# A recurrent attention kernel in which TensorE does one more matmul on constants after four groups of every step

## The chip, the cores and the metric

The kernel runs on one core of a Trainium2 chip. The metric is the time of one execution on the device, in microseconds (us): 1889.78 us is the median of three runs before the change (1886.13 to 1891.63).

## The reference

Two parts follow each other. The first is a recurrence over 768 positions, for 4 batches of 8 heads, on a 40 x 40 state; the second is a mixture of 8 experts on 3072 tokens of 320 numbers, in which all experts are computed for all tokens and weighted with a matrix that is normalised by rows and columns eight times. All is fp32.

```python
for t in range(S):
    y[:, :, t] = np.einsum('bhd,bhde->bhe', rt, state)
    Sa = np.einsum('bhde,bhe->bhd', state, at)
    state_decay = state * wt[:, :, None, :] - np.einsum('bhd,bhe->bhde', Sa, bt)
    state = state_decay + np.einsum('bhd,bhe->bhde', vt, kt)
...
x = np.ascontiguousarray(attn_out.transpose(0, 2, 1, 3)).reshape(B * S, H * D)
...
for e in range(E):
    h = np.maximum(x @ w1[e], 0.0)
    ye = h @ w2[e]
    out += P[:, e:e + 1] * ye
```

## The kernel before

**The attention** cuts the 768 positions into 12 chunks of 64. A *step* is one chunk of one batch, so there are 48. A step treats the 8 heads as 4 pairs, and each of its matmul groups is 4 matmuls (or transposes), one per pair, into one PSUM bank. The function `recur` (L235 to L302) issues a step:

- `av` (L251): the incoming state against the positions; VectorE masks it into `f` (L252)
- `xc` (L259): two groups, `xc0` and `xc1`, in a bank each; ScalarE copies them to `x1` and `c1` (L265, L266)
- `pu` (L270): `x1` through the inverted triangular matrix `tt`; VectorE masks it into `pm` (L272)
- `c2` (L277): `pm` through `bb`; VectorE adds `c1` to give `ws` (L279); GpSimd makes `y`, which goes to memory (L281), and `z`, the outgoing state (L292; on VectorE from chunk 9 on)
- `zt` (L297): `z` transposed; ScalarE copies it to `vz` (L299, L300), the incoming state of the batch's next chunk. The last chunk has none, so there are 44 of these.

These banks come from one pool of 4 (`PC`). A group of 4 x 104 columns fills 416 of a bank's 512 fp32 columns.

Around the steps stand other jobs: the loads and scans of a step's inputs and two more matmul groups, `ll` (L145) and `kt` (L153), in `prep`; the inversion of the triangular matrices on VectorE, for two chunks of all batches at a time (`inv_diag`, `inv_off`, `contract`, L170 to L182); `tload` and `tmat`, which complete the inverse with short matmuls `gp` (L226) and `op` (L231); and the experts' gate `lp` (L307), one short matmul at a time between those of `xc`.

What sets the order: a list of events sorted by due time (L346 to L382) issues the jobs, with the four batches staggered by `SKEW`; then a scheduler, which works on a model of the engines' times, lays down each engine's order. Every engine runs its order strictly. So an instruction more on TensorE also shifts what the scheduler puts where, on every engine.

**The experts** follow (from L450): matmuls at L545 and L610, with ScalarE and VectorE between them. From its eighth block on (`N_MAN`) this part has its order written out by hand.

The constants are in `cst`, [128, 660], which is loaded once at the start; its columns 232 to 359 are the identity.

Of the kernel before, what the change touches and what calls it, by code (L numbers as in the profile page):

```python
# [11 lines left out]
F32 = mybir.dt.float32  # L12
# [8 lines left out]
NP = 4  # L21
R2 = 104
# [6 lines left out]
def attention(ctx, tc, d, xd, ps, pq, pt, gs, lg):  # L29
    nc = tc.nc  # L30
    pin = ctx.enter_context(tc.tile_pool(name="a_in", bufs=1))
    inv = ctx.enter_context(tc.tile_pool(name="a_inv", bufs=1))
    sets = [ctx.enter_context(tc.tile_pool(name=f"a_set{i}", bufs=1)) for i in range(NSX)]
    const = ctx.enter_context(tc.tile_pool(name="a_const", bufs=1))
# [4 lines left out]
    cst = const.tile([128, 64 + 64 + 104 + 128 + 40 + 260], F32, name="cst")  # L39
# [7 lines left out]
    NTB = 2  # L47
    sx_b, bb_b, g_b, cc_b = ([None] * NSX for _ in range(4))
    raws = {}
    for n in range(NCH * NB - NSX, NCH * NB):  # L50
        i, pool = n % NSX, sets[n - NCH * NB + NSX]
        if i in IN_SETS or i in KB_SETS:
# [28 lines left out]
    def clear():  # L81
# [4 lines left out]
        for t in tt_b:  # L86
            nc.gpsimd.memset(t, 0.0)
    fresh = set(range(NSX))

# [9 lines left out]
    def rot(key, lst):  # L99
        i = state[key]  # L100
        state[key] = (i + 1) % len(lst)
        return lst[i]
# [3 lines left out]
    def prep(c, b, ld):  # L106
# [12 lines left out]
        sx = rot("sx", sx_b)  # L119
        i = next(j for j in range(NSX) if sx_b[j] is sx)  # L120
        g, bb, cc = g_b[i], bb_b[i], cc_b[i]
# [97 lines left out]
    def tmat(c, half):  # L219
# [12 lines left out]
        nc.scalar.copy(out=tt[0:32, :, 32:64], in_=op[0:32])  # L232
        nc.scalar.copy(out=tt[64:96, :, 96:128], in_=op[32:64])

    def recur(c, b):  # L235
        pp = preps[c, b]
        vz, zc = vz_cur[b], zp[b]
        nc.sync.dma_start(out=vz[:, :, 0:64], in_=d["v"][c, b])
        rb = io.tile([R2, NP, 128], F32, name="rb", bufs=NRB)
        nc.sync.dma_start(out=rb, in_=d["r"][c, b])  # L240
        f = wk.tile([R2, NP, 2, 104], F32, name="f", bufs=NFB)
        nc.sync.dma_start(out=f[0:64].rearrange("s p h x -> s (p h) x")[:, :, 64:104],
                          in_=d["vt"][c, b].rearrange("s (g x) -> s g x", x=40))
        if zc is None:
            nc.gpsimd.memset(f[64:104].rearrange("s p h x -> s (p h) x")[:, :, 64:104], 0.0)
        else:
            nc.scalar.copy(out=f[64:104, :, 0, 64:104], in_=zc[0:40])
            nc.scalar.copy(out=f[64:104, :, 1, 64:104], in_=zc[64:104])
        av = ps.tile([R2, NP, 2, 64], F32, name="av", tag="ps")
        for p in range(NP):  # L250
            nc.tensor.matmul(av[:, p], lhsT=vz[:, p], rhs=rb[:, p], start=True, stop=True)  # L251
        nc.vector.tensor_tensor(  # L252
            out=f[:, :, :, 0:64], in0=av,
            in1=mask_f.unsqueeze(1).unsqueeze(1).broadcast_to([R2, NP, 2, 64]), op=ALU.mult)
        yield
        xc = [ps.tile([R2, NP, 104], F32, name=f"xc{h}", tag="ps") for h in range(2)]
        for h in range(2):
            for p in range(NP):
                nc.tensor.matmul(xc[h][:, p], lhsT=pp["sx"][:, p, h], rhs=f[:, p, h], start=True, stop=True)  # L259
                if p % 2:  # L260
                    gate_step()
        x1 = wk.tile([128, NP, 104], F32, name="x1")
        c1 = rot("c1", c1_b)
        for h in range(2):
            nc.scalar.copy(out=x1[h * 64:h * 64 + 64], in_=xc[h][0:64])  # L265
            nc.scalar.copy(out=c1[h * 64:h * 64 + 40], in_=xc[h][64:104])  # L266
        yield
        pu = ps.tile([128, NP, 104], F32, name="pu", tag="ps")
        for p in range(NP):
            nc.tensor.matmul(pu[:, p], lhsT=tts[c][:, b * NP + p], rhs=x1[:, p], start=True, stop=True)  # L270
        pm = wk.tile([128, NP, 104], F32, name="pm")
        nc.vector.tensor_tensor(out=pm, in0=pu, in1=mask_p.unsqueeze(1).broadcast_to([128, NP, 104]),  # L272
                                op=ALU.mult)
        yield
        c2 = ps.tile([R2, NP, 104], F32, name="c2", tag="ps")
        for p in range(NP):
            nc.tensor.matmul(c2[:, p], lhsT=pp["bb"][:, p], rhs=pm[:, p], start=True, stop=True)  # L277
        ws = wk.tile([R2, NP, 104], F32, name="ws")
        nc.vector.tensor_tensor(out=ws, in0=c2, in1=c1, op=ALU.add)  # L279
        y = wk.tile([R2, NP, 64], F32, name="y", bufs=NY)  # L280
        nc.gpsimd.tensor_tensor(out=y, in0=ws[:, :, 0:64], in1=pp["g"], op=ALU.mult)  # L281
        col = (b % 2) * 192 + (c % 3) * 64
        tok = (c // 3) * 768 + (col // 128) * 256 + (b // 2) * 128 + col % 128
        for h in range(2):
            nc.sync.dma_start(
                out=xd[h * 160:h * 160 + 160].rearrange("(p e) t -> e p t", e=40)[:, :, tok:tok + 64],
                in_=y[h * 64:h * 64 + 40])
        gq.append(gate(c, b, y))
        if c + 1 == NCH:
            return  # L290
        z = wk.tile([R2, NP, 40], F32, name="z", bufs=4)
        (nc.vector if c >= 9 else nc.gpsimd).tensor_tensor(out=z, in0=ws[:, :, 64:104],  # L292
                                in1=preps[c + 1, b]["cc"].unsqueeze(2).broadcast_to([R2, NP, 40]), op=ALU.mult)
        yield
        zt = ps.tile([40, NP, 104], F32, name="zt", tag="ps")
        for p in range(NP):
            nc.tensor.transpose(zt[:, p], z[:, p], ident[0:R2, 0:R2])  # L297
        vz = rot("vz", vz_b)
        nc.scalar.copy(out=vz[0:40, :, 64:104], in_=zt[:, :, 0:40])  # L299
        nc.scalar.copy(out=vz[64:104, :, 64:104], in_=zt[:, :, 64:104])  # L300
        zp[b] = z
        vz_cur[b] = vz  # L302

    def gate(c, b, y):
        lp = pt.tile([64, E], F32, name="lp", tag="pt")
        for p in range(NP):
            nc.tensor.matmul(lp, lhsT=y[:, p], rhs=gs[:, p], start=(p == 0), stop=(p == NP - 1))  # L307
            if p < NP - 1:
                yield
        col = (b % 2) * 192 + (c % 3) * 64  # L310
        o = col % 128
        nc.vector.tensor_copy(out=lg[o:o + 64, c // 3 * NT + b // 2 * 3 + col // 128], in_=lp)
        yield

    def gate_step():
        if len(gq) > GL:
            next(gq[0])
            gcount[0] += 1
            if gcount[0] % NP == 0:
                gq.popleft()  # L320
# [27 lines left out]
    def step(c, b):  # L348
        if (c, b) not in gens:
            gens[c, b] = recur(c, b)  # L350
        next(gens[c, b], None)
# [6 lines left out]
    for c in range(NCH):  # L358
        for b in range(NB):
            for k in range(5):  # L360
                ev.append((5 * c + k + SKEW * b, step, (c, b)))
        t = 5 * c + 2 - T_LEAD
        ev.append((t - L_LEAD, tload, (c,)))
        for half in range(2):
            ev.append((t + 2 * SKEW * half, tmat, (c, half)))
    for s, cs in enumerate(GROUPS):
# [3 lines left out]
        for i in range(n):  # L370
            cb = (cs[0] + i // NB, i % NB)
            j = cb[0] * NB + cb[1] - NSX
            t = 5 * (j // 4) + 3 + SKEW * (j % 4) + 0.01
            t = max(t, t0 + P0 + PD * i) if s else -20 + 0.01 * i
# [16 lines left out]
PD = 0.75  # L391
INV_DT = 0.05
SKEW = 1.1
NSX = 17
GL = 3
NY = 4
# [32 lines left out]
def body(ctx, tc, d, out):  # L429
# [12 lines left out]
    with ExitStack() as actx:  # L442
        ps, pq, pt = (actx.enter_context(tc.tile_pool(name=f"a_ps{i}", bufs=n, space=bass.MemoryType.PSUM))
                      for i, n in enumerate((PC, PQ, PT)))
        nc.sync.dma_start(out=gs, in_=d["gate"])
        attention(actx, tc, d, xd, ps, pq, pt, gs, lg)
        nc.gpsimd.memset(ones, 1.0)
        nc.sync.dma_start(out=ident, in_=d["cst"][:, 232:360])
# [361 lines left out]
```

## Time and profile before

| | |
|---|---|
| median of three runs | 1889.78 us (1886.13 to 1891.63) |
| the profiled execution | 1890.4 us, span 1888.6 us, mean granted TensorE clock 0.944 |
| TensorE matmuls busy | 1768.8 us (94%), 12035 records |
| VectorE busy | 1397.3 us (74%) |
| ScalarE busy | 854.1 us (45%) |
| GpSimd busy | 876.9 us (46%) |

A span is the time from the first to the last instruction of the profiled execution; the rest of its time lies around it. The profile calls TensorE's matmuls PE and its weight loads PEld, VectorE DVE, ScalarE ACT and GpSimd POOL. Busy time of PE counts a matmul from start to modelled end, so neighbours overlap; what a matmul costs in a row of them is the distance from one start to the next. A matmul of fp32 leaves two matmul records, a transpose one. The granted clock is what share of TensorE's full speed the throttle let through: here it is always 1.0 or 0.5. In a row of waits stand who waited, for whom, the sum in us, how often, and the longest. In a row of the chain of waits stand start, length, and the number of records.

### The profile page before, as it was taken

Reading aid. Unit: us, or ns where it says so; the run is one execution under the profiler, and the core shown is the slowest. Engines: PE = TensorE matmul, PEld = TensorE weight load, DVE = VectorE, ACT = ScalarE, POOL = GpSimd, SP = SyncE. Lnnn points to the kernel's source line nnn. Section 1 sums busy time; section 2 is a strip of 40 time slices with the busy share of each in tenths; the row PEclk is TensorE's granted clock in tenths of the full one; section 3 lists DMA queues with packets and bytes.
Section 4 is the critical chain, followed back from the end, with each engine's and each line's share of the span. In section 5 each row is a group of like instructions: output and inputs, shape, how many; then the busy total and the mean of one; then the engine's idle time right before and its main releaser. Section 6 shows DMA issues by size and latency. Waiting matters only on the chain.

```text
span 1888.6 us, 31821 instructions
## 1 busy us (share of the span) xinstructions
PE 1768.8 (94%) x12035; PEld 1731.0 (92%) x12035; DVE 1397.3 (74%) x2330; ACT 854.1 (45%) x1845; POOL 876.9 (46%) x845
## 2 busy tenths in 40 slices
PE   4468989899898999999999999999999999999999
PEld 4367888889888999999999999999999999999999
DVE  7767767696579877776867777886776767777676
ACT  5346656665563444343433434345343433434342
POOL 6535445542255255371835528004462826537170
PEclk8569968988899999999999999999999999999999
DMA  8567766865642011110201102111110201111011
GB/s 191 100 133 151 151 140 134 166 137 119 147 117 70 23 51 37 37 56 19 73 21 53 52 22 74 55 33 37 37 55 19 73 19 55 37 37 56 18 37 42
DMA packets 187838, 136.26 MB, mean 72 GB/s; under 512 B 155941, under 2 KB 165285, under 8 KB 187685
## 3 DMA queue, kind: packets, MB, share of 16 engines
q1 hardware_dynamic: 184485, 128.98, 27.8%
q10 hardware_dynamic: 3200, 5.25, 1.1%
q8 instruction: 95, 1.56, 0.4%
q14 instruction: 58, 0.48, 0.1%
HBM read 113.74 MB, written 20.45 MB: 71 GB/s over the span
## 4 chain that ended last, share of the span: by engine, by line
PE 76%; DVE 7%; issue 2%; DMA 2%; POOL 1%; ACT 1%; SPq 0%; DVEq 0%; POOLq 0%; ACTq 0%
PE op L610 35%; PE p L545 32%; PE xc L259 2%; PE pu L270 1%; PE av L251 1%; PE ll L145 1%; PE c L277 1%; PE lp L307 1%; PE gp L226 1%; PE op L231 1%; DVE hl L569 1%; DVE un L182 1%; DVE gt L182 1%; PE zt L297 0%; DMA rb<-in_r_dram 0%
## 5 line engine op out<-in xcount | busy, mean ns | idle before, releaser
L545 PE MATMUL p<-xch,wh 128*128 128x384 f32 (+1 forms) x1792 | 605.0, 339 | 5.2 <-DVE cs L654 1.8
L566 ACT ACTIVATE hh<-sm 128x384 fp32r<-128x384 f32 x512 | 269.5, 526 | 726.5 <-DVE sm L563 726.5
L610 PE MATMUL op<-wh,hh 128*128 128x320 f32 x1536 | 477.4, 311 | 1.0 <-ACT hh L566 0.9
L610 PE MATMUL op<-wl,hh 128*128 128x320 f32 x1536 | 474.9, 310 | 0.0
L610 PE MATMUL op<-wh,hl 128*128 128x320 f32 x1536 | 468.1, 310 | 4.4 <-DVE hl L569 4.3
L491 POOL TENSOR_TENSOR wl<-ws,wh 128x640 fp32r<-128x640 f32 x60 | 103.3, 1721 | 608.4 <-ACT wh L489 608.2
L569 DVE SCALAR_TENSOR_TENSOR hl<-sm,hh 128x384 fp32r<-128x384 f32 x512 | 370.9, 758 | 2.8 <-ACT hh L566 2.5
L545 PEld LDWEIGHTS p<-xch,wh 128*128 128x128 f32 (+1 forms) x1792 | 337.5, 188 | 8.5 <-DVE u L563 2.7
L545 PE MATMUL p<-xcl,wh 128*128 128x384 f32 x896 | 302.8, 338 | 0.0
L545 PE MATMUL p<-xch,wl 128*128 128x384 f32 x896 | 302.2, 337 | 0.0
L610 PEld LDWEIGHTS op<-wh,hh 128*128 128x128 f32 x1536 | 290.6, 189 | 1.6 <-ACT hh L566 1.5
L610 PEld LDWEIGHTS op<-wh,hl 128*128 128x128 f32 x1536 | 287.2, 188 | 5.4 <-DVE hl L569 5.2
L610 PEld LDWEIGHTS op<-wl,hh 128*128 128x128 f32 x1536 | 291.5, 190 | 0.0
L563 DVE TENSOR_TENSOR sm<-p,u 128x384 f32<-128x384 f32 x384 | 232.8, 616 | 9.2 <-PE p L545 0.4
L545 PEld LDWEIGHTS p<-xcl,wh 128*128 128x128 f32 x896 | 168.8, 188 | 0.0
L545 PEld LDWEIGHTS p<-xch,wl 128*128 128x128 f32 x896 | 168.7, 188 | 0.0
L563 DVE TENSOR_TENSOR sm<-p,p 128x384 f32<-128x384 f32 x128 | 71.3, 557 | 130.1 <-PE p L545 76.3
L563 DVE TENSOR_TENSOR p<-p,p 128x384 f32<-128x384 f32 x128 | 71.2, 556 | 101.6 <-PE p L545 101.1
L563 DVE TENSOR_TENSOR u<-p,p 128x384 f32<-128x384 f32 x128 | 70.9, 554 | 59.3 <-PE p L545 58.0
L145 PE MATMUL ll<-ab,kb 104*128 104x128 f32 x336 | 63.4, 348 | 46.8 <-POOL ab L140 20.9
L499 POOL TENSOR_TENSOR wl<-ss,wh 128x512 fp32r<-128x512 f32 x60 | 90.7, 1512 | 33.5 <-ACT wh L496 29.3
L145 PEld LDWEIGHTS ll<-ab,kb 104*128 104x128 f32 x336 | 55.1, 249 | 51.3 <-POOL ab L140 27.1
(161 smaller groups left out, 2825.1 us busy)
## 6 DMA issues: line engine op xcount, KB each, us to landing
ws<-in_wts_dram SPq DMA_DIRECT2D x60, 832.0 KB
inp<-in_inp_dram SPq DMA_DIRECT2D x42, 521.6 KB
rb<-in_r_dram SPq DMA_DIRECT2D x48, 208.0 KB
ld<-lt ACTq DMA_DIRECT2D x40, 128.0 KB
vz<-in_v_dram SPq DMA_DIRECT2D x48, 104.0 KB
f<-in_vt_dram SPq DMA_DIRECT2D x48, 80.0 KB
xd<-y SPq DMA_DIRECT2D x96, 40.0 KB
st<-in_inp_dram SPq DMA_DIRECT2D x6, 521.6 KB
```

Source lines behind the costliest of these rows:

```text
L145: nc.tensor.matmul(ll[:, p], lhsT=kb[:, p], rhs=ab[:, p], start=True, stop=True)
L182: nc.vector.tensor_reduce(out=dst, in_=prv.rearrange("u c k r -> u c r k"), op=ALU.add, axis=AX.X)
L226: nc.tensor.matmul(gp[:, p], lhsT=lb[:, p], rhs=t1[:, p], start=True, stop=True)
L231: nc.tensor.matmul(op[:, p], lhsT=gs[:, p], rhs=t2[:, p], start=True, stop=True)
L259: nc.tensor.matmul(xc[h][:, p], lhsT=pp["sx"][:, p, h], rhs=f[:, p, h], start=True, stop=True)
L491: g.tensor_tensor(out=wl[:, 0:640], in0=raw[:, 256:896], in1=wh[:, 0:640], op=ALU.subtract)
L499: g.tensor_tensor(out=lv[:, 3:7], in0=so[:, :, 0], in1=hv[:, 3:7, 0], op=ALU.subtract)
L545: nc.tensor.matmul(o, lhsT=w_, rhs=x_, start=(j == 0), stop=(j == 3))
L563: eng.tensor_tensor(out=out, in0=x, in1=y, op=ALU.add)
L566: nc.scalar.activation(out=hh[:, f, h], in_=sm[f][:, h], func=AF.Relu)
L569: v.scalar_tensor_tensor(out=hl[:, f, h], in0=sm[f][:, h], scalar=0.0, in1=hh[:, f, h], op0=ALU.max, op1=ALU.subtract)
L610: nc.tensor.matmul(ops[i], lhsT=a[:, h, cs], rhs=w_[:, cw], start=(f == 0 and h == 0 and j == 0), stop=(last and h == 1 and j == 2))
```

## The change

`bank` gives the four tiles all 512 columns of their bank and returns the part of 416 columns that the group uses. `spin` issues one matmul (`NSPIN` is 1) of 128 rows into the unused columns 416 to 511, partitions 0 to 39, of that bank: 40 columns of the constants as weights, 96 columns of the constants as moving operand. Nothing reads its result. It is called after the groups `xc1`, `pu`, `c2` and `zt`, ahead of their readers.

```diff
+    def bank(rows, name):
+        t = ps.tile([rows, 512], F32, name=name, tag="ps")
+        return t, t[:, 0:416].rearrange("r (p x) -> r p x", p=NP)
+
+    def spin(t):
+        for _ in range(NSPIN):
+            nc.tensor.matmul(t[0:40, 416:512], lhsT=cst[:, 232:272], rhs=cst[:, 232:328], start=True, stop=True)
+
...
-        xc = [ps.tile([R2, NP, 104], F32, name=f"xc{h}", tag="ps") for h in range(2)]
+        xf, xc = zip(*(bank(R2, f"xc{h}") for h in range(2)))
...
+        spin(xf[1])
...
-        pu = ps.tile([128, NP, 104], F32, name="pu", tag="ps")
+        puf, pu = bank(128, "pu")
...
+        spin(puf)
...
-        c2 = ps.tile([R2, NP, 104], F32, name="c2", tag="ps")
+        c2f, c2 = bank(R2, "c2")
...
+        spin(c2f)
...
-        zt = ps.tile([40, NP, 104], F32, name="zt", tag="ps")
+        ztf, zt = bank(40, "zt")
...
+        spin(ztf)
...
+NSPIN = 1
```

In the program, the readers of these banks (the copies and products named above) wait for the matmul on constants too. The order of TensorE's instructions moves. Before, TensorE's order from the last `xc` of the step whose inputs are prepared in the buffer `st_185` (`bb_182` is that of the batch one step ahead; `x2` counts equal instructions in a row) reads:

```order
L259 MATMUL xc_1772<-f,st_185 104x104 x2
L307 MATMUL lp<-gs,y 64x8
L251 MATMUL av<-rb,vz_197 104x128 x4
L226 MATMUL gp<-td,lg 64x32 x8
L297 MATMUL zt<-cst,z 40x104 x4
L277 MATMUL c_1834<-pm,bb_182 104x104
L145 MATMUL ll<-ab_194,kb 128x128 x4
L153 MATMUL kt<-cst,kb 128x104 x4
L277 MATMUL c_1834<-pm,bb_182 104x104 x3
L270 MATMUL pu<-x_1787,tt_190 128x104 x3
L231 MATMUL op<-td,lg 64x32 x8
```

In the changed kernel the same piece, from the last `xc` of the same step, has a matmul on constants (L241) behind each group:

```order
L267 MATMUL xc_1805<-f,st_185 104x104 x2
L319 MATMUL lp<-gs,y 64x8
L241 MATMUL xc_1805<-cst 40x96
L259 MATMUL av<-rb,vz_197 104x128 x4
L226 MATMUL gp<-td,lg 64x32 x8
L145 MATMUL ll<-ab_194,kb 128x128 x4
L153 MATMUL kt<-cst,kb 128x104 x4
L308 MATMUL zt<-cst,z 40x104 x4
L241 MATMUL zt<-cst 40x96
L287 MATMUL c_1869<-pm,bb_182 104x104 x4
L231 MATMUL op<-td,lg 64x32 x8
L241 MATMUL c_1869<-cst 40x96
```

`ll` and `kt` moved from the middle of `c2` to ahead of `zt`, and `op` from behind `pu` to between `c2` and its matmul on constants.

In 181 of the 188 places the matmul on constants stands right behind its group or behind one gate matmul; in seven there is more between. One of the five with `ll` and `kt` between, on TensorE, is this, behind `pu` of the batch whose step is prepared in `st_188`:

```order
L279 MATMUL pu<-x_2160,tt_191 128x104 x4
L145 MATMUL ll<-ab_195,kb 128x128 x4
L153 MATMUL kt<-cst,kb 128x104 x4
L241 MATMUL pu<-cst 40x96
L267 MATMUL xc_2238<-f,st_189 104x104 x4
L267 MATMUL xc_2239<-f,st_189 104x104 x4
L241 MATMUL xc_2239<-cst 40x96
```

Before, TensorE's order at that group is:

```order
L277 MATMUL c_2139<-pm,st_187 104x104 x2
L270 MATMUL pu<-x_2114,tt_191 128x104 x4
L259 MATMUL xc_2189<-f,st_189 104x104 x4
L259 MATMUL xc_2190<-f,st_189 104x104 x4
L226 MATMUL gp<-td,lg 64x32 x8
```

`pm`, the reader of `pu`, comes free there behind `pu` itself in the kernel before, and behind `ll`, `kt` and the matmul on constants in the changed one.

## The prediction

> **What bounds the kernel now.** I read first the head of the page, then the busy time by stage, then the stretches in which TensorE's clock was halved, then what stood ahead of each of them. The head of the page:
>
> ```profile
> span 1888.6 us, 31821 instructions
> PEclk8569968988899999999999999999999999999999
> ```
>
> The clock row is low only in its first quarter. In the busy time by stage (each column: busy us, then instructions in brackets; behind POOL the granted clock, the DMA share and GB/s) the cuts are the first rise of the clock that lasts and the end of the attention:
>
> ```profile
> core 0: us, PE busy (x) PEld busy (x) DVE busy (x) ACT busy (x) POOL busy (x), PEclk, DMA share, GB/s
> 0.00:125.44 125.44, 57.83 (x315) 52.62 (x316) 88.78 (x144) 54.57 (x134) 64.78 (x88) 0.65 0.72 144
> 125.44:560.00 434.56, 396.87 (x3514) 370.11 (x3514) 317.89 (x483) 264.42 (x656) 201.82 (x230) 0.87 0.67 141
> 560.00:1888.00 1328.00, 1314.11 (x8211) 1308.25 (x8209) 990.59 (x1705) 535.10 (x1056) 610.26 (x527) 1.00 0.13 43
> ```
>
> The last 1328 us are the experts, at clock 1.00 with TensorE busy 99% of the time: the change doesn't touch them, they only start earlier or later. The first 125 us are preparations, where TensorE is idle more than half of the time. What the change touches lies in the 434.56 us between: TensorE busy for 91% of them, VectorE for 73%, and the clock at 0.87. So here TensorE sets most of the pace, and both its work and its clock count. How the lost clock is spread, in the same view cut at the changes of the clock (two stretches, and the sum over all 14 of this stage):
>
> ```profile
> 238.08:258.56 20.48, 19.90 (x112) 18.94 (x113) 15.15 (x18) 8.37 (x22) 7.11 (x10) 0.50 0.65 121
> 272.22:292.70 20.48, 20.23 (x123) 19.11 (x121) 6.02 (x11) 8.48 (x22) 5.04 (x7) 0.50 0.88 167
> sum 109.22, PE 105.58 PEld 101.43 DVE 61.94 ACT 52.01 POOL 35.13; mean PE 7.54 PEld 7.25 DVE 4.42 ACT 3.72 POOL 2.51
> ```
>
> For 109.22 us the array ran at half clock, and TensorE was busy for 105.58 of them: it had a backlog. All at full clock, that work would take 105.58/2 = 52.8 us less. What stood in the 3.41 us ahead of a fall of the clock (four single windows, then the sum over those ahead of all 14):
>
> ```profile
> 183.47:186.88 3.41, 0.87 (x8) 0.81 (x9) 2.84 (x5) 1.57 (x4) 1.49 (x3) 1.00 0.91 162
> 234.67:238.08 3.41, 1.12 (x8) 0.91 (x8) 3.41 (x5) 2.58 (x6) 3.00 (x2) 1.00 0.34 65
> 268.81:272.22 3.41, 2.02 (x28) 1.88 (x27) 1.28 (x2) 3.12 (x9) 1.99 (x3) 1.00 0.78 124
> 449.71:453.12 3.41, 3.41 (x38) 3.00 (x37) 2.49 (x10) 2.65 (x7) 0.75 (x2) 1.00 0.76 149
> sum 47.74, PE 27.76 PEld 24.55 DVE 37.44 ACT 31.03 POOL 24.99; mean PE 1.98 PEld 1.75 DVE 2.67 ACT 2.22 POOL 1.78
> ```
>
> The mean is 1.98 us busy of 3.41, where the stage has 3.12 (396.87/434.56 x 3.41): the clock falls behind a window with little array work. The window at 449.71 is wholly busy but with 38 matmul records, short ones, so what counts seems not to be the busy column but how long operands stream. Six of the 14 windows are starved: TensorE ran at most 1.47 us in each, while VectorE was busy nearly all the time. Their sum, and the sum over the six half-clock stretches behind them:
>
> ```profile
> sum 20.46, PE 7.21 PEld 6.26 DVE 19.62 ACT 11.83 POOL 10.90; mean PE 1.20 PEld 1.04 DVE 3.27 ACT 1.97 POOL 1.82
> sum 54.59, PE 52.49 PEld 50.06 DVE 37.99 ACT 27.73 POOL 20.84; mean PE 8.75 PEld 8.34 DVE 6.33 ACT 4.62 POOL 3.47
> ```
>
> So half of the lost clock (54.59 us) follows starved windows, and half (109.22 - 54.59 = 54.63 us) follows eight windows with 1.94 to 3.41 us of work, nearer to staying up.
>
> **The matmuls added.** One each behind xc, pu and c2 in 48 steps, and behind zt in 44: 188. The busy time by stage for xc alone and for pu alone shows how many stand in the first stage (in brackets; xc has 16 records a step, pu 8):
>
> ```profile
> 0.00:125.44 125.44, 4.61 (x32) 4.46 (x32) 0.65 0.72 144
> ...
> 0.00:125.44 125.44, 2.03 (x8) 1.78 (x8) 0.65 0.72 144
> ```
>
> Two steps of xc and one of pu, so 185 of the 188 lie in the busy stage. Their price comes from matmuls of 104 columns, in the chain of waits at half and at full clock (start, us, records; a matmul of fp32 leaves two matmul records):
>
> ```profile
> 388.06 1.39 PE c L277 x8
> ...
> 398.65 1.09 PE ll L145 x8
> 399.74 0.36 PE kt L153 x4
> ...
> 405.85 0.73 PE c L277 x8
> ```
>
> Four matmuls take 0.73 us at full clock, 0.1825 each; the new one streams 96 columns instead of 104: 0.1825 x 96/104 = 0.168 us. At half clock 1.39/4 x 96/104 = 0.321 us. How many fall into half clock: c2's matmuls have this busy time in the 14 stretches and in the whole stage:
>
> ```profile
> sum 109.22, PE 17.73 PEld 16.36; mean PE 1.27 PEld 1.17
> ...
> 125.44:560.00 434.56, 52.05 (x383) 46.65 (x384) 0.87 0.67 141
> ```
>
> Each takes twice as long there, so the share by count is (17.73/2)/(17.73/2 + 34.32) = 20.5%. With the clock as before: 38 x 0.321 + 147 x 0.168 = 12.2 + 24.7 = 36.9 us of TensorE time.
>
> **What hides them.** They cost nothing where TensorE would wait anyway for work that doesn't hang on the group they follow. Of TensorE's 434.56 - 396.87 = 37.7 us of idle time in the stage, the waits of that kind are these:
>
> ```profile
> PE gp L226 <- DMA td<-nd: 4.0, 4, 1.4
> ...
> PE av L251 <- DMA rb<-in_r_dram: 2.5, 1, 2.5
> PE xc L259 <- DVE g L118: 2.4, 3, 1.0
> PE c L277 <- ACT lt L159: 2.4, 1, 2.4
> ...
> PE ll L145 <- POOL ab L140: 2.1, 4, 0.8
> ...
> PE zt L297 <- DVE un L173: 1.6, 1, 1.6
> ```
>
> Together 15.0 us. I take 10 of them, two thirds, because in the starved windows VectorE is busy 19.62 of 20.46 us and TensorE is plainly ahead there; the bounds are 0 and 15. The other waits (for z, x1, ws, f) are on the step's own chain and come later by as much as the group does.
>
> **The wait added.** The readers of xc1, pu, c2 and zt (the copies on ScalarE, the masks and the sum on VectorE) now wait for the matmul on constants: 0.168 us, or 0.321. In line behind the reader on its engine stand the other batches' evacuations. For a batch's own chain that is four times a step, 0.67 to 1.3 us. A batch has a step every 434.56/48 x 4 = 36 us, and its chain is six matmul groups (av, xc twice, pu, c2, zt: 6 x 0.73 = 4.4 us) and ten copies and products between them, which the costliest groups put between these two (mean ns behind the bar):
>
> ```profile
> L252 DVE TENSOR_TENSOR f<-av,cst 104x512 f32<-104x512 f32 x39 | 26.4, 678 | 13.4 <-PE av L251 13.3
> ...
> L299 ACT COPY vz<-zt 40x160 f32<-40x160 f32 x36 | 10.3, 285 | 4.4 <-PE zt L297 3.6
> ```
>
> Ten by about 0.5 us are 5, so the chain is some 9 us of 36 and the wait lies in the slack. I cost it at nothing beyond TensorE's own time. In seven of 188 places the scheduler put other work between a group and its matmul on constants, in five of them ll and kt: a reader there waits 1.09 + 0.36 = 1.45 us more, 7 us at most in all if nothing covered it; I take 0.
>
> The Trainium skill's "PSUM — Partial Sum Buffer" (Terms) has a rule that speaks against this change: TensorE writing and another engine reading one bank in the same quadrant at a time is an error, so the matmul can't run beside the evacuation, it has to delay it. By that rule with no cover at all, the 10 us above would not be taken off. No row of before shows it, since nothing is written there behind a group.
>
> **The clock gained.** Each matmul on constants adds 0.168 us of streaming to a window of 3.41. A starved window with 8 records has two groups at most, so 0.34 us on 0.87 or 1.12: not near the mean. The eight others may be lifted. I take half of their 54.63 us, 27.3 us, which at TensorE's share of 105.58/109.22 are worth 27.3/2 x 0.967 = 13.2 us. Bounds: 0 and all 52.8. With 81.9 us left at half clock the share of the new matmuls there is 20.5% x 81.9/109.2 = 15.4%, so they cost 28 x 0.321 + 157 x 0.168 = 9.0 + 26.4 = 35.4 us.
>
> In the two long stretches above the clock stays at 0.50 for 20.48 us although TensorE is busy 19.90 and 20.23 of them. "TensorE: Matmul & The Clock Gate" of the Trainium skill (Part 1, What's actually happening) says a free-running window of about 3.4 us decides, and that one busy window releases the clock. The trace agrees with the window (stretches of 3.41, 6.82, 13.65, 20.48 us) and not with one being enough; by the rule alone 14 falls would be worth only 14 x 3.41/2 = 24 us (an estimate), and the sum with them all saved 35.4 - 10 - 24 = +1.4: that is the second rival below.
>
> **The sum.** 35.4 - 10 - 13.2 = +12.2 us. The profiled execution took 1890.4 us, 1.8 more than its span and 0.6 more than the median of 1889.8; from the median the forecast is **1902.0 us**. The instructions moved by the scheduler I take as 0, bounded by the 7 us of displaced readers.
>
> **The rivals.**
>
> *The clock holds (faster).* The eight falls don't come, and the long stretches behind the starved ones end in half the time, since every group in them streams more: 81.9 us leave half clock, worth 39.6 us; the matmuls then cost 9 x 0.321 + 176 x 0.168 = 32.5. 32.5 - 10 - 39.6 = -17.1: 1872.7 us. For it: windows like 268.81 are the ones ahead of long stretches. Against it: starved windows aren't TensorE's doing. It decides from about 50 us less at half clock.
>
> *Gain and price cancel (no change).* Only the eight falls are saved: 54.63/2 x 0.967 = 26.4 us; price 19 x 0.321 + 166 x 0.168 = 34.0; 34.0 - 10 - 26.4 = -2.4: 1887.4 us. For it: the two sums are alike in size. Against it: all eight must go.
>
> *The clock doesn't count them, the change doesn't do what it says (slower still).* The matmul lights 40 of 128 array columns. If what counts is area, windows don't rise; nothing is hidden, and one more stretch like those of 20.48 us comes (19.90/2 = 9.9 us): 36.9 + 9.9 = +46.8: 1936.6 us. For it: windows full of short matmuls of 64 columns fall (449.71). Against it: the operand has 128 rows, and rows may be what counts.
>
> **How the numbers follow.** A measurement tells 0.3%, 5.7 us, from no change (the three runs of before span 5.5). Forecast 0.42; clock holds 0.27; cancel 0.24; not counted 0.07. Faster 0.27, same 0.24, slower 0.49. The range goes from 1872, which leaves out about half of the faster rival, to 1922, which leaves out the last rival and a little of the forecast. The forecast alone has 1897 to 1922: its lower end is 15 us hidden instead of 10, its upper end nothing hidden (10 more) and one more long stretch at half clock (9.9 more).
>
> **What would show it.** In the profile after: matmul records on constants 376, about 84 ns apart at full clock; TensorE's busy time up by some 30 us before the experts; the half-clock sum of the stage at 82 us (under 35: the clock holds; over 109: not counted); the six starved windows still there, with VectorE busy; the experts' stage unchanged in length. I am wrong if the stage gets shorter, or if it grows by more than the matmuls' own time.

## The result, and the profile after

The changed kernel takes 1963.29 us (median of 4 runs, 1953.91 to 1966.09); the kernel before, run beside it, has 1887.95 us. The ratio is 1.040 (95% interval 1.035 to 1.044): **75 us slower**, where 12 were forecast, and 41 us above the top of the range.

The head of the page after:

```profile
span 1964.3 us, 32570 instructions
PE 1878.1 (96%) x12411; PEld 1789.4 (91%) x12411; DVE 1395.9 (71%) x2330; ACT 854.7 (44%) x1845; POOL 869.0 (44%) x845
PEclk8558999877777999999999999999999999999999
```

From here on *the busy stage* runs from the first `pu` to the last `c2`, so that each kernel is cut at the same events. The busy time by stage, with the columns as in the prediction: first this stage before, much like the prediction's cut at 125.44, then the three stages after:

```profile
119.55:560.03 440.48, 402.78 (x3544) 376.02 (x3544) 322.29 (x498) 267.15 (x662) 201.82 (x230) 0.87 0.67 141
```

```profile
0.00:118.18 118.18, 52.94 (x286) 47.57 (x287) 84.84 (x128) 51.94 (x129) 64.96 (x88) 0.66 0.73 149
118.18:637.75 519.57, 514.01 (x3918) 436.74 (x3918) 318.00 (x498) 267.47 (x662) 193.16 (x230) 0.81 0.57 119
637.75:1964.00 1326.25, 1311.10 (x8209) 1305.09 (x8208) 993.02 (x1705) 535.31 (x1056) 610.88 (x527) 1.00 0.13 43
```

The preparations and the experts are about as long as before (118.18 and 1326.25 us, where before had 119.55 and 1328). The busy stage grew from 440.48 to 519.57 us, by 79.1, and that is the result. In it TensorE has 3918 - 3544 = 374 more records, two for each of 187 matmuls on constants (one lies ahead of it), and is busy for 111.2 us more (514.01 - 402.78). Its idle time went from 37.7 to 5.6 us. Its clock went **down**, from 0.87 to 0.81. VectorE, ScalarE and GpSimd have as many instructions as before.

The stretches at half clock in that stage after (four of 8, then the sum of all 8), and the sum of the 15 of before:

```profile
118.18:166.87 48.69, 48.69 (x249) 41.77 (x250) 30.50 (x46) 16.68 (x42) 11.62 (x14) 0.50 0.33 68
...
375.08:412.63 37.55, 37.55 (x191) 31.97 (x192) 15.66 (x37) 14.99 (x38) 9.58 (x14) 0.50 0.59 115
...
508.20:532.09 23.89, 23.89 (x122) 19.69 (x121) 13.43 (x13) 7.03 (x18) 1.69 (x3) 0.50 0.20 44
...
573.05:614.01 40.96, 40.96 (x219) 34.87 (x220) 18.98 (x35) 20.14 (x44) 21.07 (x19) 0.50 0.45 121
sum 195.46, PE 195.29 PEld 165.83 DVE 107.04 ACT 80.80 POOL 57.29; mean PE 24.41 PEld 20.73 DVE 13.38 ACT 10.10 POOL 7.16
```

```profile
sum 115.11, PE 111.47 PEld 107.32 DVE 66.31 ACT 54.70 POOL 35.13; mean PE 7.43 PEld 7.15 DVE 4.42 ACT 3.65 POOL 2.34
```

The first stretch of each kernel reaches in from the preparations, so the clock fell 7 times in the stage instead of 14. But the stretches last longer: up to 48.69 us at half clock with a TensorE that is busy all the time, and 195.46 us in all instead of 115.11. What stood in the 3.41 us ahead of the 7 falls (the emptiest window, a full one, then the sum over all 7):

```profile
371.67:375.08 3.41, 2.18 (x25) 1.81 (x23) 2.75 (x3) 0.86 (x3) 3.04 (x4) 1.00 0.98 166
...
569.64:573.05 3.41, 3.41 (x35) 2.90 (x35) 0.50 (x1) 2.35 (x5) 0.62 (x2) 1.00 0.82 128
sum 23.87, PE 20.41 PEld 17.03 DVE 17.31 ACT 7.63 POOL 9.75; mean PE 2.92 PEld 2.43 DVE 2.47 ACT 1.09 POOL 1.39
```

No fall comes behind a starved window any more (the prediction expected all six to stay), and four of the seven windows are busy throughout.

What one matmul on constants costs is read from the timeline of TensorE, at full clock (start, us, engine, line, operation, tiles, records):

```profile
241.92 0.98 PE L287 MATMUL c<-pm,st 128*104 128x104 f32 x8
242.82 0.36 PE L241 MATMUL c<-cst 128*40 128x96 f32 x2
243.11 1.14 PE L279 MATMUL pu<-x,tt 128*128 128x104 f32 x8
```

From the first matmul of `c2` to the first of `pu` it takes 243.11 - 241.92 = 1.19 us; the four matmuls of `c2` alone take 0.73, as the prediction's row has it. The matmul on constants costs 0.46 us, not 0.168.

### The profile page after: what moved, and what is told of

It is laid out like the page before. It is cut to its first block, busy times and chain, and to the rows that moved or that the text cites. A ratio compares the mean times of both kernels' runs of the same rounds, so it can differ in the third digit from the quotient of the medians.

```text
span 1964.3 us, 32570 instructions
## 1 busy us (share of the span) xinstructions
PE 1878.1 (96%) x12411; PEld 1789.4 (91%) x12411; DVE 1395.9 (71%) x2330; ACT 854.7 (44%) x1845; POOL 869.0 (44%) x845
## 4 chain that ended last, share of the span: by engine, by line
PE 84%; DVE 6%; DMA 4%; POOL 2%; issue 2%; ACT 1%; SPq 1%; ACTq 0%; DVEq 0%; POOLq 0%
PE op L623 33%; PE p L558 31%; PE xc L267 4%; PE pu L279 3%; PE av L259 2%; DMA inp<-in_inp_dram 2%; PE c L287 2%; PE ll L145 1%; PE lp L319 1%; PE gp L226 1%; PE op L231 1%; PE zt L308 1%; DMA ld<-lt 1%; DVE hl L582 1%; DMA lu<-ld 1%
```

## The experiments

Two theories after the result. **W, the switch:** a matmul with few weight columns (40) next to ones with 104 or 128 makes TensorE pause on both sides. The kernel before has this already, around the gate's matmuls with 64 weight columns. Its chain of waits (start, us, records):

```profile
394.32 0.21 PE lp L307 x2
394.53 0.54 PE xc L259 x4
395.08 0.21 PE lp L307 x2
...
400.83 0.89 PE pu L270 x8
401.72 0.37 PE xc L259 x4
```

Four records of `xc` take 0.37 us among their like, and 0.54 between two of the gate's: 0.17 more per visit. (The row of `pu` is for later: 0.89 us for eight records.) **P, the place:** any matmul put behind a group into its bank costs 0.4 us. The runs of before beside the experiments have medians from 1884.6 to 1889.7 us; each ratio is to those.

**The number of weight columns.** Three kernels are edited in the columns of the weights alone: 104, 72 and 64 for 40 (with as many rows in the result; the bank of `zt` is allocated with 104 rows for it). By the traces, TensorE's order stays nearly that of the changed kernel with 64 and 72 columns, and is another with 104.

```diff
-            nc.tensor.matmul(t[0:40, 416:512], lhsT=cst[:, 232:272], rhs=cst[:, 232:328], start=True, stop=True)
+            nc.tensor.matmul(t[0:104, 416:512], lhsT=cst[:, 232:336], rhs=cst[:, 232:328], start=True, stop=True)
```

> The matmul on constants with 104 weight columns instead of 40 (same 96 moving columns, same places; its result fills 104 partitions). Theory W (a switch between matmuls of at most 64 weight columns and wider ones leaves TensorE about 93 ns idle going in and 84 to 91 ns coming out at full clock, as xc to lp 185 against 92 ns already shows before): no extra gap at the new matmuls, xc1 to constants 92 ns, constants to the next group 92 ns; 188 x 0.184 = 35 us of TensorE time at full clock and some 45 at the granted one, of which about 30 fills idle time; time 1890 to 1920 us. Rival P (any matmul put behind a group into its bank costs 0.4 us, for its weights or its bank): gaps of 175 to 205 ns stay, time 1955 to 1975 us.

> The matmul on constants with 72 weight columns. Theory W with the border above 64: like 104 columns, no gaps, 1888 to 1920 us. Rival G (the gap grows with the difference in columns to the neighbour): gaps in between, 130 to 150 ns where 185 stood, 1920 to 1945 us. Rival P: 1955 to 1975 us.

> The matmul on constants with 64 weight columns. Theory W with the border above 64: gaps as with 40 columns (185 ns in, 175 out), time 1945 to 1980 us. Rival G: gaps of 140 to 160 ns, 1925 to 1950 us. If it is like 104 columns, the border lies between 40 and 64.

Measured: 104 columns 1897.09 us (ratio 1.0048, 1.0020 to 1.0076); 72 columns 1919.89 us (1.0154, 1.0106 to 1.0201); 64 columns 1961.23 us (1.0397, 1.0346 to 1.0448), the same as 40. TensorE's timeline at full clock with 104, with 72 and with 64 columns:

```profile
260.31 0.90 PE L267 MATMUL xc<-f,st 104*104 104x104 f32 x8
261.05 0.34 PE L241 MATMUL xc<-cst 128*104 128x96 f32 x2
261.22 1.05 PE L259 MATMUL av<-rb,vz 104*104 104x128 f32 x8
```

```profile
273.18 0.90 PE L287 MATMUL c<-pm,st 128*104 128x104 f32 x8
273.91 0.33 PE L241 MATMUL c<-cst 128*72 128x96 f32 x2
274.08 0.62 PE L279 MATMUL pu<-x,tt 128*128 128x104 f32 x4
```

```profile
302.87 1.14 PE L279 MATMUL pu<-x,tt 128*128 128x104 f32 x8
303.93 0.38 PE L241 MATMUL pu<-cst 128*64 128x96 f32 x2
304.24 0.61 PE L267 MATMUL xc<-f,sx 104*104 104x104 f32 x4
```

Eight records and the matmul on constants take 0.91 us with 104 columns and 0.90 with 72: 0.18 and 0.17 more than the 0.73 of eight alone, which is what the prediction had priced. With 64 columns, behind `pu` (0.89 us without), they take 1.37: 0.48 more. So W holds, with its border between 64 and 72 columns, and P and a price that grows with the difference fall. From 64 to 72 columns, with nearly the same order, the kernel gets 41 us faster. The busy stage with 104 columns, for later:

```profile
117.53:568.84 451.31, 429.90 (x3917) 400.11 (x3918) 314.82 (x498) 267.89 (x662) 195.01 (x230) 0.91 0.67 137
```

The half-clock sums in the busy stage were 79.30 us with 104 columns, 130.78 with 72 and 207.75 with 64; each such sum is from the one profiled execution of its kernel. That 72 columns took 23 us more than 104 isn't the matmul's price, which is the same. It is the clock: half of the 51 us more at half clock is about that much, and over all runs of the two the mean clock is 0.946 against 0.956. Why the clock fell more is open; TensorE's order differs between the two.

**The switches of the kernel before.** Here there are no matmuls on constants; the gate's matmuls get 72 weight columns instead of 64, and the 8 rows of result too many are not read.

```diff
-        y = wk.tile([R2, NP, 64], F32, name="y", bufs=NY)
+        yw = rot("y", yb)
+        y = yw[:, 0:NP * 64].rearrange("r (p t) -> r p t", p=NP)
...
-            nc.tensor.matmul(lp, lhsT=y[:, p], rhs=gs[:, p], start=(p == 0), stop=(p == NP - 1))
+            nc.tensor.matmul(lp, lhsT=y[:, p * 64:p * 64 + 72], rhs=gs[:, p], start=(p == 0), stop=(p == NP - 1))
```

> The kernel before, without matmuls on constants; the gate's matmuls (lp) read 72 weight columns instead of 64, 8 of them the neighbour's or zero, and 64 of the 72 result rows are used. 140 switches fewer in TensorE's order (122 instead of 262). Theory W: 140 x 0.09 = 12 us of TensorE time less, xc to lp at 92 ns instead of 185 and lp to xc near 60 instead of 132; time 1870 to 1884 us, faster by 0.2 to 0.9%. Rival P (no cost of narrow weights as such): 1888 us within 5, the gaps at lp stay.

Measured: 1914.91 us, **slower** by 1.2% (ratio 1.012, 1.007 to 1.017), where W expected 0.2 to 0.9% less. The timeline of TensorE and the busy stage:

```profile
202.91 0.24 PE L309 MATMUL lp<-gs,yb 104*72 104x8 f32 x2
203.00 0.59 PE L260 MATMUL xc<-f,st 104*104 104x104 f32 x4
203.43 0.24 PE L309 MATMUL lp<-gs,yb 104*72 104x8 f32 x2
```

```profile
121.45:581.62 460.17, 406.29 (x3508) 386.56 (x3509) 322.90 (x493) 266.62 (x661) 197.65 (x230) 0.82 0.63 135
```

The price of a switch went away as W has it: one visit of the gate and four records of `xc` take 203.43 - 202.91 = 0.52 us instead of 0.21 + 0.54 = 0.75. But TensorE then waited for 460.17 - 406.29 = 53.9 us instead of 37.7, and the clock was at 0.82 instead of 0.87, with 161.31 us at half. Less work on TensorE, more waiting, a lower clock: here the time follows the clock more than the work. That the saved work itself lowered the clock isn't shown: TensorE's order moved too, and its 46 us more at half clock (161.31 - 115.11) are no more than the 51 between 104 and 72 columns.

**Streaming between the switches.** Two kernels keep the switches of the change and alter what streams between them: 8 moving columns instead of 96, and two matmuls on constants at each place instead of one.

```diff
-            nc.tensor.matmul(t[0:40, 416:512], lhsT=cst[:, 232:272], rhs=cst[:, 232:328], start=True, stop=True)
+            nc.tensor.matmul(t[0:40, 416:424], lhsT=cst[:, 232:272], rhs=cst[:, 232:240], start=True, stop=True)
```

> The matmul on constants of the change with 40 weight columns, but only 8 moving columns instead of 96: it costs two switches and almost no streaming. Theory W (the switches are the price): 188 places x (93 + 84 + 2 x 40 to 58) = 0.26 to 0.29 us against 0.38 to 0.42 with 96 columns, so 49 to 55 us of TensorE time at full clock, about 30 of it in idle time; and the gaps let the array idle, so half clock in the busy stage stays above the 115 us of before: 1915 to 1950 us. Rival S (the 96 streamed columns are the price, the gaps matter little): 1885 to 1900 us.

```diff
-NSPIN = 1
+NSPIN = 2
```

> The change with two matmuls on constants (40 weight columns, 96 moving) at each place instead of one: as many switches, twice the streaming between them. At full clock the second costs about 2 x 0.09 to 0.11 = 0.2 us, 188 x 0.2 = 38 us. Theory W with the clock as shown by the 8-column run (switches with little streaming between them keep the array at half clock): half clock in the busy stage falls from 195 us to 90 to 150, time 1965 to 1995 us. Rival (the half-clock time follows TensorE's total load, not the idle at switches): half clock 195 us or more, the second costs 0.2 to 0.35 us throughout, time 2005 to 2035 us.

Measured: with 8 columns 2018.49 us (ratio 1.069, 1.063 to 1.076), 55 us more than the change itself; with two matmuls 1965.18 us (1.041, 1.035 to 1.048), the same as with one. The half-clock sums of the busy stage, first for 8 columns, then for two matmuls:

```profile
309.48:401.64 92.16, 92.16 (x501) 83.75 (x500) 53.47 (x77) 38.70 (x98) 27.57 (x35) 0.50 0.49 98
...
sum 388.55, PE 386.77 PEld 346.73 DVE 205.19 ACT 150.09 POOL 114.00; mean PE 38.68 PEld 34.67 DVE 20.52 ACT 15.01 POOL 11.40
```

```profile
sum 87.40, PE 84.73 PEld 71.61 DVE 44.47 ACT 41.22 POOL 26.15; mean PE 8.47 PEld 7.16 DVE 4.45 ACT 4.12 POOL 2.62
```

With 8, 96 and twice 96 columns at the same places: 388.55, 195.46 and 87.40 us at half clock. The busy column can't see the difference, it says 92.16 of 92.16 us in the longest stretch. Differences of 193 and 108 us are far above the 46 to 51 seen with a moved order. So the clock goes by what streams, and the pauses of the switches seem to count as idle for it. Both theories' times for 8 columns were too low by over 65 us, since neither let the clock fall that far. For two matmuls the half clock came out a little below W's 90 to 150 and far from the rival's 195, and the time at W's lower end: the second matmul pays for itself through the clock.

**Rows.** This is the kernel with 104 weight columns, in the same order, with 72 rows of operands instead of 128.

```diff
-            nc.tensor.matmul(t[0:104, 416:512], lhsT=cst[:, 232:336], rhs=cst[:, 232:328], start=True, stop=True)
+            nc.tensor.matmul(t[0:104, 416:512], lhsT=cst[0:72, 232:336], rhs=cst[0:72, 232:328], start=True, stop=True)
```

> The matmul on constants with 104 weight columns as in w104, the same order, but 72 rows of operands instead of 128: the same time on TensorE, less of the array lit. Theory R (the clock follows streamed rows; a window at half clock must be about three quarters of 128 rows full to end it): half clock in the busy stage rises from 79 us to 90 to 120, time 1900 to 1915 us. Rival T (it follows streaming time alone): half clock 70 to 90 us, time 1890 to 1902 us.

Measured: 1905.98 us (ratio 1.0088, 1.0056 to 1.0120) against 1.0048 (1.0020 to 1.0076) with 128 rows; half clock 101.87 us against 79.30. Time and clock came out as R has them, but the intervals overlap. A count over the traces points the same way. It takes the 1776 windows of 3.41 us in the busy stages of all 13 profiles and splits them by one border, fitted to them, into those with half clock in the next window and those with full. Split by the columns that stream in a window, each matmul's counted times its rows, 1726 fall on the right side; without the rows 1670; by the busy share 1337; calling every next window full gives 1251. The border lies at 0.40 of what matmuls of 128 rows would stream at full clock (128 columns in 0.112 us, as `ll` does). So that lit rows count is likely, but no run shows it by itself.

**Another order alone.** The kernel before with its batches staggered differently.

```diff
-SKEW = 1.1
+SKEW = 1.0
```

> The kernel before with SKEW 1.0 instead of 1.1: the same instructions, about 1064 lines of difference in TensorE's order. It gauges what another order alone does. If order matters little: 1888 us within 6, and the 1.0% between 104 and 72 weight columns isn't the order. If order (through where the windows of the clock fall) matters: off by 10 to 25 us in either direction, with half clock in the busy stage off from 115 us by twice that.

Measured: 1896.78 us (ratio 1.0044, 1.0016 to 1.0072), half clock 115.10 us, as before. This order costs 8 us with the same clock. In the profiled execution the three stages have 120.81, 442.42 and 1330.57 us, some 1 to 3 more in each than before, so the cost isn't in the busy stage alone. An order can do something of that size; this one does nothing like 75 us.

**Both at once, and fewer.** Three kernels combine the gate with 72 weight columns with matmuls on constants of 104: at all four places, behind `c2` and `zt` alone, and behind `xc1` and `pu` alone. The two smaller ones are the first with these lines taken out:

```diff
-        spin(xf[1])
-        spin(puf)
```

```diff
-        spin(c2f)
-        spin(ztf)
```

> Matmuls on constants with 104 weight columns, and the gate's matmuls with 72: 112 switches in TensorE's order instead of 358. Theory W: 246 x 0.09 = 22 us of TensorE time less than w104, the array idles less in windows at half clock, so half clock stays at 60 to 90 us: 1872 to 1890 us, perhaps faster than before. Theory C (less TensorE work only makes it wait more, and the clock falls more, as gate72 showed): half clock 100 to 160 us, 1890 to 1915 us.

> Gate with 72 weight columns, matmuls on constants with 104 weight columns behind c2 and zt alone (92 of them). 92 fewer than g72w104 is 92 x 0.18 to 0.2 = 17 us less TensorE time. If what they stream is what holds the clock (theory C): half clock in the busy stage lies between the 161 us of gate72 and the 65 of g72w104, near 110, and time stays 1880 to 1905 us. If a few suffice: half clock under 80 us and 1872 to 1885 us, faster than before.

> The same with the matmuls on constants behind xc1 and pu alone (96 of them). Theory C: like behind c2 and zt, half clock near 110 us, 1880 to 1905 us. If the place counts (xc1 and pu lie ahead of av and zt, where TensorE waits for z): half clock under 80 us here and not behind c2 and zt, 1872 to 1885 us.

Measured: 1893.05 us (ratio 1.0022, 1.0000 to 1.0044) with 65.40 us at half clock; 1901.57 us (1.0052, 1.0026 to 1.0078) with 112.40; 1894.16 us (1.0016, 0.9990 to 1.0041) with 114.58. In these profiles the half clock of the last two lies where theory C has it, between the gate alone (161.31) and all four places. The profiles hide a difference, though: behind `xc1` and `pu` the kernel is 7 us faster than behind `c2` and `zt`, and over the twelve runs of each the mean clock is 0.950 against 0.944 (the profiled run of the faster one has the lowest clock of its twelve). So the place, or the order that goes with it, counts too, by less than the rival theory had it; why is open. For the first kernel, W was right on the clock and 3 us too low at least on the time. Here the same edit of the gate did not lower the clock: 65.40 us at half against 79.30 with 104 columns and the old gate. None beats the kernel before: with the clock nearly held, the busy stage of the first is as long as before (440.26 us), so what the clock and the switches gave back is about what the 188 matmuls cost.

## Why the prediction was wrong

It forecast the right sign and a sixth of the size. Two of its own signs of being wrong came true: the half-clock sum rose above 109 us, and the stage grew by more than the matmuls' own time. By its steps:

- **What bounds the stage** was right: TensorE's work and its clock. All of the change came out of that stage, and the experts' length didn't move.
- **The matmuls added: the step that failed first.** 0.168 us each was taken from matmuls of 104 columns among their like. The matmul itself costs that (0.17 and 0.18 us with 72 and 104 weight columns), but with 40 it also costs a pause on each side: 0.46 us. 188 places by 0.46 are 86 us at full clock, instead of the 31.6 that 0.168 gives (the sum below lowers the 86). The number was there before the run: `xc` at 0.54 us instead of 0.37 beside the gate's narrow matmuls. I took a price from the middle of a group for work that stands at its border.
- **What hides them**: 10 us taken, 15 as the bound, and 37.7 - 5.6 = 32.1 measured. Nearly all of TensorE's waiting was filled, that on the step's own chain too. But this goes with the wrong price: with 104 columns, at nearly the price that was forecast, TensorE still waits for 451.31 - 429.90 = 21.4 us, so 16.3 were filled, close to the bound.
- **The wait added** at nothing: nothing shows against it. With 104 columns the same readers wait at the same places, and the whole kernel is 9 us slower.
- **The instructions moved** at nothing. Not counting the matmuls on constants, TensorE changes between matmuls of at most 64 weight columns and wider ones (transposes taken as wide) 352 times in the busy stage after and 256 times before. At half of 0.17 us each the 96 more are some 8 us, an estimate.
- **The clock gained: the step that failed by as much.** I took 27 us less at half clock, a gain of 13.2 us; there were 80 more (195.46 - 115.11), a loss of about 40 us at half the work. Of its two parts one was right: the falls became fewer. But I had priced only falls, and took it for granted that a stretch ends as before. By the runs with 8 and twice 96 columns, a stretch ends when enough streams, and the pauses took that away.
- **The sum of what was measured:** 86 for the matmuls with their pauses, 40 for the clock, 32 hidden, is +94, where the stage shows +79.1. Two terms are too high, by these rows of after (at full clock, then at half):

```profile
249.01 0.28 PE L319 MATMUL lp<-gs,y 104*64 104x8 f32 x2
249.22 0.61 PE L267 MATMUL xc<-f,st 104*104 104x104 f32 x4
249.76 0.28 PE L319 MATMUL lp<-gs,y 104*64 104x8 f32 x2
249.90 0.34 PE L241 MATMUL xc<-cst 128*40 128x96 f32 x2
250.17 1.12 PE L259 MATMUL av<-rb,vz 104*104 104x128 f32 x8
```

```profile
127.94 1.71 PE L287 MATMUL c<-pm,bb 128*104 128x104 f32 x8
129.58 0.54 PE L241 MATMUL c<-cst 128*40 128x96 f32 x2
130.05 2.04 PE L279 MATMUL pu<-x,tt 128*128 128x104 f32 x8
```

  Behind a gate matmul, which is narrow too, the matmul on constants adds no switch: 250.17 - 249.76 = 0.41 us against 249.22 - 249.01 = 0.21, so 0.20. In 64 of the 188 places just one neighbour is a matmul with 64 weight columns; 124 by 0.46 and 64 by 0.20 are 70 us, and with the 8 for the moved order 78. And at half clock a place costs 130.05 - 127.94 - 1.39 = 0.72 us, not twice 0.46. Adding up, over all records of both traces, the distance to the next record that their kind has at full clock gives 80 us more work and 35 us lost to the clock. 80 + 35 - 32 is +83, within 4 us of the stage.
- **The rivals:** "the clock doesn't count them" came nearest (1936.6, chance 0.07), for a wrong reason. It took the area lit by the 40 columns to be too small; with two of the same matmuls at each place the clock holds. The rule of the "TensorE: Matmul & The Clock Gate" page of the Trainium skill (Part 1, What's actually happening), that one busy window of some 3.4 us releases the clock, fits only if "busy" means streamed operands: a TensorE busy 40.96 of 40.96 us by the profile stayed at 0.50.

## What to carry to other kernels

Price an added instruction by its neighbours: look for a place in the trace where its kind (here, few weight columns) already stands next to the kind it will stand beside, and read the distance from start to start across that border. An engine that the profile calls busy may still be pausing, and where a clock follows the work that is done, pauses cost twice. A filler that is to hold a clock has to look like the work around it; even then, in none of these kernels did it earn more than it cost.

## What the runs showed of the hardware

- Between matmuls of at most 64 and of at least 72 weight columns, fp32, TensorE pauses on both sides: 0.46 to 0.48 us for a matmul of 96 columns at full clock instead of 0.17 to 0.18. Transposes with 40 columns don't do this: the `c2` at 405.85 us in the prediction's rows has 0.73 us, and in the same chain of waits it stands right behind `zt`:

```profile
405.49 0.36 PE zt L297 x4
405.85 0.73 PE c L277 x8
```

- The granted clock can stay at 0.50 for 92 us while the profile calls TensorE busy without a break (the run with 8 columns).
- Taking the gate's switches off TensorE went with a lower clock and a kernel 1.2% slower (that one caused the other isn't shown). Doubling the change's matmuls on constants cost nothing: 1965.18 us against 1963.29, with 87.40 us at half clock instead of 195.46.
